# A two-layer attention decode on one core: value products with the probabilities as weights, one-unit loads around the change of batch, and smaller portions of side work

## The chip, the cores and the metric

The kernel runs on one core of a Trainium2 chip. The metric is the time of one execution on that core in microseconds (us). Every comparison below uses fast runs: the granted TensorE clock was 1.00.

## The reference

One new token is decoded for each of eight sequences, through the same attention and feed-forward block twice. Keys and values of 8 sequences x 32 heads x 4096 positions x 128 channels in bf16 are what has to be read: 134 million numbers of each, a second time for the second layer where they are no longer on the chip.

```python
B, Sq, D = 8, 1, 640
Hq, Hkv, Sk, Dh = 32, 32, 4096, 128          # Dff = 1728
...
def reference(A_x, A_k_cache, A_v_cache, A_wq, A_wo, B_x, B_w1, B_w2):
    def _A_ref(x, k_cache, v_cache, wq, wo):
        q = ...                                # x @ wq, one row per head
        scores = jnp.einsum("bhqd,bhkd->bhqk", q, k) * (Dh ** -0.5)
        p = _softmax(scores, axis=-1)
        o = jnp.einsum("bhqk,bhkd->bhqd", p, v)
        return ... @ wo
    def _B_ref(x, w1, w2): ...                 # max(x @ w1, 0) @ w2
    x = A_x
    x = x + _A_ref(_layernorm(x, axis=-1), A_k_cache, A_v_cache, A_wq, A_wo)
    x = x + _B_ref(_layernorm(x, axis=-1), B_w1, B_w2)
    x = x + _A_ref(_layernorm(x, axis=-1), A_k_cache, A_v_cache, A_wq, A_wo)
    x = x + _B_ref(_layernorm(x, axis=-1), B_w1, B_w2)
    return x
```

Both layers read the same cache, and sequences (the text calls each a batch) do not touch each other.

## The kernel before

All weights stay in SBUF. Beside them lies an arena of 22 units of 512 KB, through which the cache streams. The work goes in visits: a visit is one pair of heads of one batch in one layer, with four units of keys and then four of values. A planner in plain Python lays down every load, product and side step in order. Because layer 1 reads what layer 0 has read, the last 16 units of a batch in layer 0 are not freed but used again by layer 1. From then until layer 1 has used them the stream has only 22 - 16 = 6 units to live in. That happens once for each of the eight batches, and the text calls it a dip, after what the transfer rate does there.

The size of a load follows the room that is left:

```python
GPH = 2; UNIT = 2 * GPH; GP = 4; G = 22; SPARE = 6; SMALL = 4; AHEAD = 3   # one line each
...
            keeping = keeps(which, i, g)
            roomy = G - len(kept)
            n = 4 if keeping or roomy >= 16 else 2 if roomy >= SMALL else 1
```

Side work (layer norms, feed-forward, queries of layer 1, output products) waits in chains. Between attention blocks the planner takes one step off every chain, whatever its size:

```python
    def step():
        for c in chains:
            if c:
                ops.append(c.pop(0)[1])
                rest(c)
        ...
        small = G - len(kept) < SMALL
        for g in range(UNIT):
            ops.append(("mm", which, i, g, find(which, i, g)))
            release(which, i, g)
            if g + 1 < UNIT and (g % 2 or small):
                step()
```

One such step may be a whole half of the feed-forward (70 products), or 40 query products. Keys and values both are the stationary operand of TensorE, with one moving column:

```python
        for n in range(GJ):                     # 16 products for each unit
            j = half * GJ + n
            lhsT = arena[:, u * GW + n * P : u * GW + (n + 1) * P]
            if which == "K":
                nc.tensor.matmul(s_tiles[i][:, h, j : j + 1], lhsT=lhsT, rhs=q, start=True, stop=True)
            else:
                nc.tensor.matmul(
                    oy[i][:, h : h + 1], lhsT=lhsT, rhs=P_tiles[i][:, h, j : j + 1],
                    start=(j == 0), stop=(j == NJ - 1),
                )
```

The root of the layer norm is one activation on ScalarE (`func=ACT.Sqrt`), which needs another table than the exponentials (the trace has 49 table loads, 1.28 us each).

## Time and profile before

| | before |
|---|---|
| median of 4 runs | 2524.14 us |
| span of the profiled run | 2523.4 us |
| moved | 1027.07 MB, mean 407 GB/s |
| granted clock | 1.00 |

First, from the page, the busy time of each engine with its share and its number of instructions, and the queue that carries the instructions themselves (packets, MB, share of the 16 transfer engines).

```profile
PE 1385.3 (55%) x40134; PEld 1300.3 (52%) x40134; DVE 320.3 (13%) x1707; ACT 287.9 (11%) x1422; POOL 0.7 (0%) x6
...
q8 instruction: 313, 5.13, 0.8%
```

TensorE has 40,134 products and as many weight loads.

Then the timeline of TensorE in the dip of which the prediction shows the feed-forward part, a little later (start, duration, engine, line, operation, output and inputs, number merged; in brackets the idle time before it and what ended it).

```profile
535.79 1.23 PE L385 MATMUL q_ps<-xq,wq_sb 128*128 128x1 bf16 x40
538.13 0.99 PE L411 MATMUL s_ps<-q,arena 128*128 128x1 bf16 x32 [1.12 <-ACT q L396]
...
542.01 0.37 PE L385 MATMUL q_ps<-xq,wq_sb 128*128 128x1 bf16 x8 [1.61 <-issue]
```

Forty query products stand in one block, the keys wait 1.12 us for the copy behind them, and in the middle of a later block of forty TensorE stands still for 1.61 us with nothing that it is seen to wait for.

### The profile page before, as it was taken

What the parts mean: (1) busy time and instruction counts of PE and PEld (TensorE: products, weight loads), DVE (VectorE), ACT (ScalarE), POOL (GpSimd) and SP (SyncE); (2) the same over time, 40 slices, a digit from 0 to 9 for tenths busy, and PEclk for the clock granted to TensorE, in tenths of its full rate; (3) what the DMA queues carried; (4) which work ended last, traced back from release to release, by engine and by line L of the source; (5) the groups of instructions that cost most, each with busy time, mean ns of one, the idle gap of its engine ahead of it and who ended that gap; (6) DMA issues with size and microseconds to landing.
All of it is one profiled execution on the core that took longest, in us unless ns stands there. A gap on an engine that the chain in (4) does not pass through costs nothing.

```text
span 2523.4 us, 84569 instructions
## 1 busy us (share of the span) xinstructions
PE 1385.3 (55%) x40134; PEld 1300.3 (52%) x40134; DVE 320.3 (13%) x1707; ACT 287.9 (11%) x1422; POOL 0.7 (0%) x6
## 2 busy tenths in 40 slices
PE   3447545475454755557455564555645466445745
PEld 3336545464454744547454564545645455444744
DVE  0001111111111111111111111111111111111111
ACT  1001101010010101101010110101101011000200
POOL 0000000000000000000000000000000000000000
DMA  9999999999999999999999999999999999999897
GB/s 408 425 426 377 414 425 426 424 353 426 426 425 419 362 425 425 425 408 380 426 425 426 395 366 426 425 426 389 402 425 425 425 377 405 426 425 409 325 425 307
DMA packets 82525, 1027.07 MB, mean 407 GB/s; under 512 B 9220, under 2 KB 9220, under 8 KB 9220
## 3 DMA queue, kind: packets, MB, share of 16 engines
q1 hardware_dynamic: 82180, 1021.68, 97.3%
q8 instruction: 313, 5.13, 0.8%
q14 instruction: 32, 0.26, 0.0%
HBM read 1021.63 MB, written 0.01 MB: 405 GB/s over the span
## 4 chain that ended last, share of the span: by engine, by line
DMA 76%; PE 19%; issue 4%; ACT 1%; SPq 0%; DVE 0%; ACTq 0%
DMA arena<-in_A_k_cache_dram 38%; DMA arena<-in_A_v_cache_dram 38%; PE s_ps L411 6%; PE oy_ps L413 6%; PE blk_ps L448 1%; PE q_ps L385 1%; DMA wq_sb<-in_A_wq_dram 1%; PE oy_ps L463 1%; PE ch_ps L334 1%; PE ch_ps L351 1%; PE blk_ps L424 1%; ACT L442 0%; PE blk_ps L433 0%; PE ch_ps L312 0%; ACT P_sb L442 0%
## 5 line engine op out<-in xcount | busy, mean ns | idle before, releaser
L411 PE MATMUL s_ps<-q,arena 128*128 128x1 bf16 x16384 | 518.0, 165 | 586.3 <-DMA arena<-in_A_k_cache_dram 530.4
L413 PE MATMUL oy_ps<-P_sb,arena 128*128 128x1 bf16 x16384 | 520.0, 166 | 509.8 <-DMA arena<-in_A_v_cache_dram 482.8
L411 PEld LDWEIGHTS <-arena 128*128 128x128 bf16 x16384 | 479.7, 104 | 607.6 <-DMA arena<-in_A_k_cache_dram 547.9
L413 PEld LDWEIGHTS <-arena 128*128 128x128 bf16 x16384 | 481.8, 105 | 555.5 <-DMA arena<-in_A_v_cache_dram 500.6
L437 ACT ACTIVATE nmax<-blk_ps 128x2 f32<-128x2 f32 x256 | 44.0, 172 | 1985.0 <-PE blk_ps L433 1985.0
L452 DVE RECIPROCAL invL<-blk_ps 128x2 f32<-128x2 f32 x256 | 43.7, 171 | 966.0 <-PE blk_ps L448 966.0
L428 DVE TENSOR_REDUCE hmx<-blk_ps 2x1 f32<-2x128 f32 x256 | 71.4, 279 | 732.3 <-PE blk_ps L424 732.3
L448 PE MATMUL blk_ps<-lrow,ones_c 128*128 128x2 f32 x512 | 145.3, 353 | 2.5 <-issue 2.5
L442 ACT ACTIVATE P_sb<-s_ps,nmax 128x32 bf16<-128x32 f32 x512 | 142.2, 283 | 7.8
L463 PEld LDWEIGHTS <-wo_sb 128*128 128x128 bf16 x2560 | 131.7, 121 | 7.4 <-issue 7.2
L448 PEld LDWEIGHTS blk_ps<-lrow,ones_c 128*128 128x128 f32 x512 | 128.7, 311 | 4.2 <-issue 2.6
L463 PE MATMUL oy_ps<-oT,wo_sb 128*128 128x1 bf16 x2560 | 104.9, 165 | 6.6 <-issue 5.4
L442 ACT ACTIVATION_READ_ACCUMULATOR P_sb<-s_ps,nmax 128x1 f32 x512 | 100.5, 196 | 0.0
L420 DVE TENSOR_REDUCE mrow<-s_ps 128x2 bf16<-128x64 f32 x256 | 57.6, 225 | 214.3 <-PE s_ps L411 214.3
L424 PE MATMUL blk_ps<-ident,mrow 128*2 128x128 bf16 x256 | 68.4, 267 | 1.5 <-issue 1.3
L456 DVE TENSOR_TENSOR oT<-oy_ps,invL 128x2 bf16<-128x2 f32 x256 | 40.8, 159 | 159.5 <-PE oy_ps L413 159.5
L385 PEld LDWEIGHTS <-wq_sb 128*128 128x128 bf16 x1440 | 43.2, 105 | 14.1 <-issue 10.8
L351 PEld LDWEIGHTS <-w_sb 128*128 128x128 bf16 x1120 | 45.3, 107 | 8.7 <-issue 6.6
L351 PE MATMUL ch_ps<-hT,w_sb 128*128 128x1 bf16 x1120 | 45.9, 168 | 6.1 <-issue 5.7
L470 DVE TENSOR_TENSOR xT<-xT,oy_ps 128x5 f32<-128x5 f32 x256 | 41.0, 160 | 46.8 <-PE oy_ps L463 25.4
L433 PE MATMUL blk_ps<-diag,onesb_c 2*128 2x2 bf16 x256 | 46.8, 183 | 0.0
L385 PE MATMUL q_ps<-xq,wq_sb 128*128 128x1 bf16 x1280 | 40.0, 165 | 10.3 <-issue 10.3
(42 smaller groups left out, 324.7 us busy)
## 6 DMA issues: line engine op xcount, KB each, us to landing
arena<-in_A_v_cache_dram SPq DMA_DIRECT2D x208, 2048.0 KB, 21.9
arena<-in_A_k_cache_dram SPq DMA_DIRECT2D x192, 2048.0 KB, 22.5
arena<-in_A_k_cache_dram SPq DMA_DIRECT2D x96, 1024.0 KB, 8.5
arena<-in_A_v_cache_dram SPq DMA_DIRECT2D x64, 1024.0 KB, 7.1
wq_sb<-in_A_wq_dram SPq DMA_DIRECT2D x4, 1280.0 KB, 25.0
wo_sb<-in_A_wo_dram SPq DMA_DIRECT2D x4, 1280.0 KB, 34.3
w_sb<-in_B_w_dram SPq DMA_DIRECT2D x1, 2240.0 KB, 36.6
w_sb<-in_B_w_dram SPq DMA_DIRECT2D x1, 2160.0 KB
```

What stands on the lines that cost most here:

```text
L351: nc.tensor.matmul(y_ps[:, c : c + 1], lhsT=w2_sb[:fs, f, c * P : (c + 1) * P], rhs=st[key, "hT"][:fs, f : f + 1], start=(f == 0), stop=(f ...
L385: nc.tensor.matmul(q_ps[:, h, :], lhsT=wq_sb[:, g, c, h * Dh : (h + 1) * Dh], rhs=xl[:, c : c + 1] if layer else xl[:, :, c], start=(c == ...
L411: nc.tensor.matmul(s_tiles[i][:, h, j : j + 1], lhsT=lhsT, rhs=q, start=True, stop=True)
L413: nc.tensor.matmul(oy[i][:, h : h + 1], lhsT=lhsT, rhs=P_tiles[i][:, h, j : j + 1], start=(j == 0), stop=(j == NJ - 1),)
L420: nc.vector.tensor_reduce(out=m_tiles[i], in_=s_tiles[i], axis=AX.X, op=ALU.max)
L424: nc.tensor.matmul(blk[i][:2, :P], lhsT=m_tiles.pop(i), rhs=ident, start=True, stop=True)
L428: nc.vector.tensor_reduce(out=hmx, in_=blk[i][:2, :P], axis=AX.X, op=ALU.max)
L433: nc.tensor.matmul(blk[i][:, P : P + 2], lhsT=ones_b, rhs=nmax.pop(i), start=True, stop=True)
L437: nc.scalar.activation(out=nm, in_=blk[i][:, P : P + 2], func=ACT.Copy, scale=-inv_sqrt_dh)
L442: nc.scalar.activation(out=P_tiles[i][:, h, :], in_=S[:, h, :], func=ACT.Exp, bias=nm[:, h : h + 1], scale=inv_sqrt_dh, accum_out=l_tiles[ ...
L448: nc.tensor.matmul(blk[i][:, P + 2 : P + 4], lhsT=ones_f, rhs=l_tiles.pop(i), start=True, stop=True)
L463: nc.tensor.matmul(oy[i][:, 2 + c : 3 + c], lhsT=wo_sb[:, 2 * hp + h, c * P : (c + 1) * P], rhs=o[:, h : h + 1], start=(h == 0), stop=(h = ...
```

## The change

The intent is to get the dips out of the transfer rate. The change has these parts, cut to their core here:

```diff
-SMALL = 4
-AHEAD = 3
+SMALL = 8
+AHEAD = 4
+CAP = 20
...
-            n = 4 if keeping or roomy >= 16 else 2 if roomy >= SMALL else 1
+            n = 4 if roomy >= 16 else 2 if roomy >= SMALL else 1
+            if i == NV - 1 and which == "V":
+                n = 1
...
     def step():
-        for c in chains:
-            if c:
-                ops.append(c.pop(0)[1])
-                rest(c)
+        n = 0
+        for c in sorted(chains, key=lambda c: c[0][0]):
+            if not n or n + c[0][0] <= CAP:
+                n += c[0][0]
+                take(c)
...
-            if g + 1 < UNIT and (g % 2 or small):
+            if g + 1 < UNIT:
                 step()
...
+        if which == "V":
+            for c in range(4):
+                h, j = c // 2, g * VJ + c % 2 * CJ
+                nc.tensor.matmul(
+                    o_ps[32 * c : 32 * c + CJ, :], lhsT=P_tiles[i][:, h, j : j + CJ],
+                    rhs=arena[:, at + c * CJ * Dh : at + (c + 1) * CJ * Dh],
+                    start=(g == 0), stop=(g == UNIT - 1), tile_position=(0, 32 * c),
+                )
+            return
...
+            if nb == 1:
+                inverse_root(rstd, st[key, "var"])     # about 12 small DVE operations
+            else:
+                ... ACT.Sqrt, reciprocal
...
+    up_parts = [range(f, min(f + 3, FC)) for f in range(0, FC, 3)]
...
+        b0, nb = (b, 1) if layer == 0 else (0, B)      # layer 1: one finish for all batches
```

In words: loads of one unit where six are free; at most 20 side products between two units, with the feed-forward cut into portions of 14 or 15 and queries into portions of 10; the first visits of the next batch that come between a batch's two layers are four instead of three; the value product uses four columns of the probabilities as weights in each of four column strips and streams the values, followed by a copy of 100x512 to SBUF and four small gathering products; the root moves from ScalarE to VectorE; the softmax sum becomes a product with ones; layer 1's output products and feed-forward are done once, for all eight batches, at the end. The array of values is laid out on the host to suit (not timed, as before).

## The prediction

> **What bounds the kernel now.** I began with the page's row of slices. It asks one question: is any engine, or the transfer system, full?
>
> ```profile
> PE   3447545475454755557455564555645466445745
> DMA  9999999999999999999999999999999999999897
> GB/s 408 425 426 377 414 425 426 424 353 426 426 425 419 362 425 425 425 408 380 426 425 426 395 366 426 425 426 389 402 425 425 425 377 405 426 425 409 325 425 307
> DMA packets 82525, 1027.07 MB, mean 407 GB/s; under 512 B 9220, under 2 KB 9220, under 8 KB 9220
> ```
>
> TensorE is half idle; the transfers are busy nine tenths of nearly every slice, and most slices stand at 425 or 426 GB/s, the plateau. 1027.07 MB at 426 GB/s are 2411.0 us, so of the span of 2523.4 us 112.4 us are transfer time lost, and no change that keeps the bytes can win more. The losses are eight dips, one in about every five slices, and the end. Next I cut the span into stretches of 40 us and looked around one dip (columns: stretch, its length, busy time of PE, PEld, DVE, ACT, POOL with instructions, granted clock, DMA share, GB/s).
>
> ```profile
> 440.00:480.00 40.00, 19.24 (x568) 18.09 (x568) 4.34 (x23) 3.27 (x20) 0.00 (x0) 1.00 1.01 425
> 480.00:520.00 40.00, 20.15 (x574) 18.66 (x570) 5.45 (x29) 4.56 (x21) 0.00 (x0) 1.00 0.95 391
> 520.00:560.00 40.00, 31.18 (x901) 29.58 (x901) 6.04 (x33) 8.43 (x31) 0.00 (x0) 1.00 0.96 356
> 560.00:600.00 40.00, 23.60 (x690) 22.02 (x686) 5.71 (x30) 4.09 (x25) 0.00 (x0) 1.00 1.00 413
> ```
>
> Where GB/s falls, PE rises to 31 of 40 us. With (426 - GB/s) / 426 x 40 us for each stretch, the eight dips cost 8.9, 11.1, 10.4, 9.3, 13.5, 8.9, 10.1 and 17.4 us: 89.6 in all. The first stretch costs 2.8, the end (2480 on) 17.6; 2.4 are spread thinly. This is the budget.
>
> Why the dips? The plan keeps 16 of the 22 arena units (512 KB each) for the second layer, so around each change of batch the stream lives in 6 units. There the kernel loads 2 units at a time, so three slots. In the same stretch TensorE must do the batch's finish (feed-forward) and the second layer's queries. The timeline of one dip:
>
> ```profile
> 523.93 9.57 SPq L376 DMA_DIRECT2D arena<-in_A_v_cache_dram  x4
> 523.94 2.25 PE L334 MATMUL ch_ps<-xf,w_sb 128*128 128x1 bf16 x70
> 524.24 1.28 ACT L442 ACT_TABLE_LOAD   x1
> 525.53 0.29 ACT L442 ACTIVATE P_sb<-s_ps,nmax 128x32 bf16<-128x32 f32 x1
> ...
> 527.43 1.38 PE L351 MATMUL ch_ps<-hT,w_sb 128*128 128x1 bf16 x33
> 529.05 1.60 PE L351 MATMUL ch_ps<-hT,w_sb 128*128 128x1 bf16 x37 [0.24 <-issue]
> ```
>
> All 70 products of one feed-forward half go out in one block, 2.25 us, then 70 more in about 3.2 us. A 2-unit attention block takes only 1.0 us, so during a block no arena unit comes free, and the queue of loads runs dry. The second cause is in the groups' idle column:
>
> ```profile
> L413 PE MATMUL oy_ps<-P_sb,arena 128*128 128x1 bf16 x16384 | 520.0, 166 | 509.8 <-DMA arena<-in_A_v_cache_dram 482.8 <-issue 26.7
> L411 PE MATMUL s_ps<-q,arena 128*128 128x1 bf16 x16384 | 518.0, 165 | 586.3 <-DMA arena<-in_A_k_cache_dram 530.4 <-issue 46.9 <-ACT q L396 8.9
> L385 PE MATMUL q_ps<-xq,wq_sb 128*128 128x1 bf16 x1280 | 40.0, 165 | 10.3 <-issue 10.3
> ```
>
> "issue" is time in which PE waited for nothing the profile shows: 84 us in these rows, in single gaps of 1 to 3 us, nearly all in the dips. My reading, which I mark as inference, is that instructions arrive late: instructions come through the same transfer engines (queue q8, 5.13 MB), and the gaps follow long runs of back-to-back PE instructions.
>
> **What the Trainium skill says.**
> "TensorE: Matmul & The Clock Gate", Part 3, says products in different column strips run at once and gives 2.38x for three strips at N=512; Part 2 gives a lone warm matmul a gap of N/2.4 + 2.5 ns, so 216 ns at N=512. "TensorEngine Tiling (Array Packing)", Performance Considerations, recommends just this swap of stationary and streaming operand when the moving side is thin. The trace before has no such product, so it can't say; its thin pairs run at 1.01 us per 32, 32 ns each.
> "ScalarE: Activation LUTs", What ACT_TABLE_LOAD costs, gives 1283 ns per load; the trace agrees exactly (49 loads, mean 1283 ns).
> "DMA: Bandwidth & Descriptors", SWDGE vs HWDGE vs iDMA, measured 408.7 GB/s for one load stream with 4 KiB rows. This trace's loads have rows of 8 and 16 KB; whole bins of 16 KB rows reach 426, the best of 8 KB rows about 420.
>
> **The change part by part.**
> *Value products turned round.* Per unit, 16 pairs (weights from V, one column) become 4 pairs (weights from P, 4 columns; moving 512 columns of V), each in its own column strip. Before: 0.52 us a unit. After: about 0.3 us if the strips overlap, 4 x 216 = 0.86 us if not (estimates from the skill). Added per visit: a copy of 100x512 by ACT (estimate 0.7 us, extrapolated from the 128x64 copy's 212 ns) and 4 thin gather pairs on PE (0.13 us plus latency). Neither lies on the load path in the steady state, where PE waits 2.3 to 2.7 us for each load.
> *PE instructions.* Listed per engine, 79,352 become 52,866. At 64 B (5.39 MB of instruction traffic over 84,569 instructions) that removes 1.7 MB, 4.0 us of plateau transfer, less a little for added DVE work: 4 us on the path, because the transfers are the path.
> *Softmax sum.* 512 fp32 passes of 353 ns become 256 bf16 products of 64 columns; 512 accumulator reads of 196 ns leave ACT; one more 0.2 us reduction per visit on DVE. All hidden.
> *Layer norm.* Square root moves from ACT to about 12 small DVE operations of about 0.16 us, 2.5 us with gaps; 46 of 49 table loads go. The plan puts an empty step behind it, but a maximum queued behind it on DVE can hold PE for about 1.7 us, twice a dip. Six single units give slack: a freed unit may return late by 5 x 1.23 us less about 1.8 us of transfer latency, about 4.3 us. So covered.
> *Second layer's finish once for all eight batches.* 7 feed-forwards (980 pairs) and 1120 output pairs go. Most lay in plateau stretches (360 to 400 us is at 425 GB/s), so they were free; only the last dip, which holds two finishes, profits.
> *Pacing.* The blocks of 70 become parts of 14 or 15, and queries come 10 at a time; at most 20 products stand between two units. PE time per unit: 0.3 to 0.5 us of attention plus up to 0.66 us, against 1.23 us per unit at 426 GB/s. Over four visits (32 units) the transfer needs 39.4 us. PE needs: K 16 x 0.52 = 8.3, V 16 x 0.3 = 4.8 (13.8 if serial), 140 + 160 pairs x 33 ns = 9.9, norms 4 x 0.57 = 2.3, small work 4. Together 29 (38 if serial). Before, the 31 us of PE in 40 us also fitted on average; it was the lumps and gaps that lost.
> *Smaller loads.* 260 loads of one unit (4 KB rows), nearly all in the dips. From the packets, 8 KB rows take 309 ns and 16 KB 613, so a row costs about 5 ns extra; with the gap per load I estimate 1.3 us per dip.
> *End.* The last values come unit by unit (saves about 1.5 us), the copy and gather cost about 1 us. 17.6 becomes about 17.
>
> Sum: bytes 1025.4 MB / 426 = 2407; start 2.8; spread 2.4; end 17; dips 8 x 2.5 = 20 (1.3 small loads, 1.2 leftover waits). That is 2449 of span; run times lie about 0.7 above. **Predicted 2450 us**, 2.9% less.
>
> **The rivals.**
> (a) *The small loads don't hold the plateau.* For: 4 KB rows at the skill's 408.7 GB/s, one issue of 0.33 us for each, 32 in a dip. Against: 0.33 is far below 1.23 us, and 8 KB rows lose little. It would cost 3 to 5 us per dip: about 2465.
> (b) *The strips don't overlap, or run at a slow array clock.* 38 of 39.4 us leaves no room for waits, so dips stay at 7 to 9 us: 2490 to 2505. Against: the skill's measured overlap, and the granted clock stands at 1.00.
> (c) *The gaps called issue stay.* They took 84 us on PE in all. If they depend on time since the last pause and not on the number of instructions, 5 us a dip remain: about 2470.
> (d) *The new copy becomes a wait.* One o_ps bank: the copy must end before the next values, one key block away, at least 2 us. Unlikely to show.
> (e) *Nothing is lost in the dips:* 2430.
>
> **Range and chances.** Most weight lies on dips of 1 to 6 us: 2435 to 2480. 2% is at about 2474, which means 5.6 us per dip; about four fifths lie below. Faster 0.82, within 2% 0.165, slower 0.015 (only if the serial strips also hurt the steady state). Range 2432 to 2482.
>
> **What would show it.** Slices at the dips should read 405 to 420 GB/s instead of 353 to 395. The idle column of the key and value products should show issue of 40 us or less in place of 74. A value unit should take 0.3 us, its four products starting nearly together; 0.8 us would prove rival (b). One-unit loads landing at clearly over 1.23 us apart with units free would prove (a). Issue gaps of the old size inside the dips would prove (c). A plateau other than 425 would overturn the whole sum.

## The result, and the profile after

| | before | after | predicted |
|---|---|---|---|
| median | 2524.65 us (13 runs, with those of later rounds) | 2467.20 us (8 runs, 2466.06 to 2468.24) | 2450 |
| ratio | | 0.9775 (0.9765 to 0.9785) | 0.971 |
| span | 2523.4 | 2464.8 | 2449 |

A ratio is the mean time of one kernel's fast runs over the mean of the other's fast runs of the same rounds, so it is not quite the ratio of the two medians. The change is faster by 2.25%, outside the 2% band, inside the predicted range (2432 to 2482), and 17 us slower than the predicted time. Of an expected gain of 74 us, 57 came. The record lists a ninth run of the kernel after, 2468.76 us, that its median leaves out.

The page after, its busy times, the rate in 40 slices, the bytes and the instruction queue:

```profile
PE 1282.4 (52%) x26486; PEld 794.4 (32%) x26486; DVE 381.5 (15%) x1984; ACT 337.3 (14%) x1179; POOL 0.7 (0%) x6
...
GB/s 406 425 426 405 420 427 425 424 397 425 426 426 423 392 426 426 426 421 397 426 427 425 413 410 427 426 426 404 411 426 426 426 405 418 426 426 412 410 425 305
DMA packets 105896, 1025.38 MB, mean 416 GB/s; under 512 B 11829, under 2 KB 11829, under 8 KB 45109
...
q8 instruction: 207, 3.39, 0.6%
```

The plateau of 425 to 427 GB/s has not moved. The eight low places are still there and read 392 to 413 where they read 325 to 395. TensorE has a third fewer products, and instructions take 1.74 MB less.

The stretches around the dip that the prediction shows (columns as there):

```profile
480.00:520.00 40.00, 23.45 (x491) 15.58 (x492) 8.54 (x47) 4.88 (x16) 0.00 (x0) 1.00 0.99 396
520.00:560.00 40.00, 34.67 (x763) 24.17 (x760) 9.57 (x52) 8.48 (x38) 0.00 (x0) 1.00 1.02 410
```

391 and 356 GB/s have become 396 and 410, though TensorE is busier there than before (34.67 of 40 us against 31.18): a fuller engine, and a better fed stream. What counts in the dip is not how much work there is but how long one piece of it can hold up the next free unit.

The budget, made as in the prediction from stretches of 40 us:

| us | before | predicted | after |
|---|---|---|---|
| bytes at 426 GB/s | 2411.0 | 2407 | 2407.0 |
| eight dips | 89.6 | 20 | 33.5 |
| start | 2.8 | 2.8 | 2.8 |
| end | 17.6 | 17 | 17.5 |
| thinly spread | 2.4 | 2.4 | 4.0 |
| span | 2523.4 | 2449 | 2464.8 |

So 13.5 of the 16 us that the span is above its prediction lie in the dips, 4.2 us for each instead of 2.5.

The value, key and query groups after (columns: busy time and mean ns, then idle time before them with its causes):

```profile
L460 PE MATMUL o_ps<-arena,P_sb 128*4 128x512 bf16 x4096 | 557.4, 606 | 579.1 <-DMA arena<-in_A_v_cache_dram 573.6
L472 PE MATMUL s_ps<-q,arena 128*128 128x1 bf16 x16384 | 536.4, 165 | 544.2 <-DMA arena<-in_A_k_cache_dram 534.0
...
L444 PE MATMUL q_ps<-xq,wq_sb 128*128 128x1 bf16 x1280 | 53.8, 166 | 3.6 <-issue 2.9
```

Next to nothing but transfers is left in the idle column. "Issue" is 2.9 us here in the queries; the list of waits adds 7.6 for the keys and 3.5 for the values (sum, number, longest):

```profile
PE s_ps L472 <- issue: 7.6, 11, 1.6
PE o_ps L460 <- issue: 3.5, 3, 2.0
```

Those 14 us stand against 84 before in the same three groups. But look at the busy time of the values: 557.4 us for 1024 units are 0.54 us a unit, no less than the 520.0 us of before.

The timeline of the dip shows both how the portions lie between units and what still holds a unit up:

```profile
514.80 0.16 PE L491 MATMUL blk_ps<-diag,onesb_c 2*128 2x2 bf16 x1 [0.95 <-DVE diag L488]
514.89 0.56 PE L376 MATMUL ch_ps<-xf,w_sb 128*128 128x1 bf16 x15
515.38 0.60 PE L460 MATMUL o_ps<-arena,P_sb 128*4 128x512 bf16 x4
515.91 0.56 PE L376 MATMUL ch_ps<-xf,w_sb 128*128 128x1 bf16 x15
516.40 0.60 PE L460 MATMUL o_ps<-arena,P_sb 128*4 128x512 bf16 x4
...
2426.68 1.02 PE L460 MATMUL o_ps<-arena,P_sb 128*4 128x512 bf16 x8
```

Fifteen feed-forward products, a unit of values, fifteen, a unit: one unit comes free about every microsecond. In front of it TensorE has waited 0.95 us for a small product on VectorE, which was queued behind the new root. The last line is from the steady state: two units of values back to back take 1.02 us, 0.51 each.

The loads after (number, KB each, median us from issue to landing):

```profile
arena<-in_A_v_cache_dram SPq DMA_DIRECT2D x132, 512.0 KB, 7.1
arena<-in_A_k_cache_dram SPq DMA_DIRECT2D x128, 512.0 KB, 7.5
```

These are the 260 one-unit loads. From the completion records in the trace I took, for each load, the time at which the last of the 16 transfer engines reported, and the distance from one load to the next where loads follow without a pause. One unit of 512 KB then takes 1.276 us in one-unit loads (rows of 4 KB), 1.2465 in two-unit loads (8 KB) and 1.226 in four-unit loads (16 KB). That sizes the tax of small loads in a dip: 32 units x 0.05 us and 24 more in pairs x 0.02 are 2.1 us. The rest of the 4.2, again 2.1 us, is what the small loads do not explain. I count it as waits here; what stays open, further down, says how much of it may be none. The prediction had 1.3 and 1.2.

### The profile page after: what moved, and what is told of

Read it like the earlier page. It is cut to its first block, busy times and chain, and to the rows that moved or that the text cites. A ratio compares the mean times of both kernels' runs of the same rounds, so it can differ in the third digit from the quotient of the medians.

```text
span 2464.8 us, 57629 instructions
## 1 busy us (share of the span) xinstructions
PE 1282.4 (52%) x26486; PEld 794.4 (32%) x26486; DVE 381.5 (15%) x1984; ACT 337.3 (14%) x1179; POOL 0.7 (0%) x6
## 2 busy tenths in 40 slices
DMA packets 105896, 1025.38 MB, mean 416 GB/s; under 512 B 11829, under 2 KB 11829, under 8 KB 45109
## 4 chain that ended last, share of the span: by engine, by line
DMA 83%; PE 13%; DVE 2%; issue 1%; ACT 0%; SPq 0%; ACTq 0%
DMA arena<-in_A_k_cache_dram 43%; DMA arena<-in_A_v_cache_dram 41%; PE s_ps L472 5%; PE o_ps L460 5%; PE q_ps L444 1%; DVE hmx L486 1%; ACT o_sb L518 0%; PE oy_ps L523 0%; PE oy_ps L540 0%; DVE diag L488 0%; PE blk_ps L491 0%; PE blk_ps L482 0%; PE blk_ps L504 0%; PE ch_ps L393 0%; PE ch_ps L376 0%
## 5 line engine op out<-in xcount | busy, mean ns | idle before, releaser
L460 PE MATMUL o_ps<-arena,P_sb 128*4 128x512 bf16 x4096 | 557.4, 606 | 579.1 <-DMA arena<-in_A_v_cache_dram 573.6
L472 PEld LDWEIGHTS <-arena 128*128 128x128 bf16 x16384 | 493.0, 104 | 578.2 <-DMA arena<-in_A_k_cache_dram 568.9
L460 PEld LDWEIGHTS <-P_sb 128*4 128x4 bf16 x4096 | 109.8, 83 | 684.6 <-issue 678.3
L518 ACT CAST o_sb<-o_ps 100x512 bf16<-100x512 f32 x256 | 149.8, 585 | 124.3 <-PE o_ps L460 124.3
L510 DVE TENSOR_REDUCE lsum<-blk_ps 128x2 f32<-128x64 f32 x256 | 57.5, 225 | 422.1 <-PE blk_ps L504 422.1
L504 PEld LDWEIGHTS <-onesb_c 128*128 128x128 bf16 x256 | 26.5, 103 | 203.7 <-issue 203.7
L523 PE MATMUL oy_ps<-gsel,o_sb 100*128 100x2 bf16 x1024 | 63.5, 166 | 3.5 <-ACT o_sb L518 0.7
L504 PE MATMUL blk_ps<-P_sb,onesb_c 128*128 128x64 bf16 x256 | 59.9, 234 | 1.1 <-ACT P_sb L499 1.1
L540 PE MATMUL oy_ps<-oT,wo_sb 128*128 128x1 bf16 x1280 | 51.8, 165 | 0.0
L540 PEld LDWEIGHTS <-wo_sb 128*128 128x128 bf16 x1440 | 50.9, 105 | 0.8 <-issue 0.8
```

Of the source, the lines that this page charges most:

```text
L460: nc.tensor.matmul(o_ps[32 * c : 32 * c + CJ, :], lhsT=P_tiles[i][:, h, j : j + CJ], rhs=arena[:, at + c * CJ * Dh : at + (c + 1) * CJ * D ...
L472: nc.tensor.matmul(s_tiles[i][:, j : j + 1], lhsT=arena[:, at + n * P : at + (n + 1) * P], rhs=q, start=True, stop=True)
L504: nc.tensor.matmul(blk[i][:, P + 2 :], lhsT=ones_p, rhs=P_tiles[i].rearrange("p h j -> p (h j)"), start=True, stop=True)
L518: nc.scalar.copy(out=o_tiles[i][:OR], in_=o_ps[:OR, :].rearrange("p (j d) -> p j d", j=CJ))
L523: nc.tensor.matmul(oy[i][:, :2], lhsT=o_tiles[i][:OR, j, :], rhs=gsel[:OR, j, :], start=(j == 0), stop=(j == CJ - 1))
L540: nc.tensor.matmul(oy[i][:, 2 + c * nb : 2 + (c + 1) * nb], lhsT=wo_sb[:, 2 * hp + h, c * P : (c + 1) * P], rhs=o1[:, 2 * hp + h, :] if la ...
```

## The experiments

Each was compared with the kernel before in the same rounds; the distance to the kernel after is between medians (2467.2). In these rounds the kernel before had medians of 2524.35 to 2525.70 us, so such a distance is good to 1 or 2 us. All results were correct. There are two questions: which part of the change earns the time, and what holds the rest of the dips.

### Single loads undone

```diff
-SMALL = 8
+SMALL = 4
```

> The changed kernel, but with two-unit loads (1 MB) in place of one-unit loads (512 KB) where the arena is short. Theory load tax: the trace after shows a unit landing every 1.276 us with one-unit loads, 1.247 with two-unit and 1.226 with four-unit loads, so 32 units a dip x 0.03 x 8 dips = 8 us are won and the time falls to about 2459 us. Theory slack: what made the dips short is that one-unit loads leave the tensor engine more slack before the queue runs dry; then the dips grow from 4.2 us to 6 to 8 us each and the time rises to 2480 to 2497 us.

Measured: 2494.69 us, ratio 0.9881 (0.9862 to 0.99): 27 us more than after. In the same dip, on TensorE:

```profile
525.42 0.62 PE L376 MATMUL ch_ps<-xf,w_sb 128*128 128x1 bf16 x10
527.72 0.60 PE L460 MATMUL o_ps<-arena,P_sb 128*4 128x512 bf16 x4 [1.67 <-DMA arena<-in_A_v_cache_dram]
```

The values now come 1.67 us late, and the stretch 520 to 560 carries 371 GB/s instead of 410. Six units in pairs are three slots, and a slot is asked for again only when both units are read. Small loads cost transfer time, and earn more than they cost.

### Single loads alone, in the kernel before

```diff
-SMALL = 4
+SMALL = 8
```

> The kernel before with one constant changed (one-unit loads, and a chain step after each unit, where under 8 units are free); all the rest as before. Theory slack: most of the gain is finer loads, so the dips fall from 11.2 to about 6 us and the time to about 2480 us. Theory lumps and gaps: the blocks of 70 products and the issue gaps remain, so the dips stay at 9 to 11 us and the time at 2505 to 2525 us.

Measured: 2549.79 us, ratio 1.0095 (1.0079 to 1.0111): 25 us slower than before, which neither theory had. In the kernel before the same constant also decides that side steps come after each unit instead of each pair, and a wait that was not there appears in the list of waits (sum, number, longest):

```profile
PE s_ps L411 <- issue: 48.8, 33, 2.5
PE blk_ps L448 <- ACT P_sb L442: 30.4, 32, 1.7
```

The softmax sum is asked for too early behind the exponentials, 32 times. The issue gaps stay, and so do the blocks of 70. So this run has two edits in one and does not price single loads cleanly. What it does show is that the constant whose undoing costs 27 us in the new kernel brings no gain in the old one, with the steps that come along with it.

### Blocks of 70 again

The cap is lifted and each half of the feed-forward is one step; queries stay in portions of 10, but nothing limits what is put together.

```diff
-CAP = 20
+CAP = 1000
...
-    up_parts = [range(f, min(f + 3, FC)) for f in range(0, FC, 3)]
-    visits, ops = plan(B, NP, len(up_parts), DC)
+    up_parts = [range(FC)]
+    visits, ops = plan(B, NP, len(up_parts), 1)      # "down" loops over c inside
```

> The changed kernel with the feed-forward in two blocks of 70 products again and no cap on the products per step. Theory pacing: the lumps made the dips; they grow from 4.2 to 7 or 8 us and the time rises to 2490 to 2500 us. Theory slack: six single units tolerate about 4 us, a block takes 2.3 to 3 us, so each block costs under 1 us: 2470 to 2480 us.

Measured: 2509.61 us, ratio 0.9937 (0.9919 to 0.9954): 42 us more than after, more than the pacing theory gave. One stretch and three lines of the timeline:

```profile
520.00:560.00 40.00, 31.69 (x720) 22.79 (x720) 8.66 (x48) 8.49 (x38) 0.00 (x0) 1.00 0.93 343
```

```profile
520.10 2.25 PE L376 MATMUL ch_ps<-xf,w_sb 128*128 128x1 bf16 x70
522.28 0.60 PE L461 MATMUL o_ps<-arena,P_sb 128*4 128x512 bf16 x4
522.81 2.83 PE L394 MATMUL ch_ps<-hT,w_sb 128*128 128x1 bf16 x70
```

TensorE does about as many products in the stretch as after (720 against 763), but only one unit comes free between 520.1 and 525.6 us, while the stream can fill four in that time (5.5 / 1.276); the rate falls to 343 GB/s. The issue gaps of TensorE came to 0.6 us in this whole run. So lumps do the harm without any help from the issue gaps. Part of the 42 us may be a further wait that this plan makes: output products up to 2.2 us behind their input, 15.5 us in seven waits.

### Values as weights again

The value product, its layout and two output buffers as before; no copy, no gather. All the rest of the change stays. The diff is shortened.

```diff
-            for c in range(4):
-                ... lhsT=P_tiles[i][:, h, j : j + CJ], rhs=arena[...512 columns...], tile_position=(0, 32 * c)
+            for n in range(GJ):
+                nc.tensor.matmul(oy[i][:, h : h + 1], lhsT=arena[:, at + n * P : at + (n + 1) * P],
+                                 rhs=P_tiles[i][:, h, j : j + 1], ...)
```

> The changed kernel with the value products as before (weights from V, one column each), layout of V as before, no copy and no gather. 24 thousand more tensor engine instructions: 1.6 MB more instruction traffic, 3.7 us of plateau, in any case. Theory issue gaps: idle put down to issue on the key and value products returns from 11 us to over 50, dips grow to 7 us, time 2490 to 2500 us. Theory that pacing alone did it: dips stay at 4 to 5 us and the time at 2470 to 2475 us.

Measured: 2508.72 us, ratio 0.9931 (0.9916 to 0.9946): 41 us more than after, above the 2490 to 2500 of the issue theory. From its list of waits, and its instruction queue:

```profile
PE s_ps L471 <- issue: 37.4, 22, 2.9
PE oy_ps L460 <- issue: 26.1, 13, 2.4
```

```profile
q8 instruction: 295, 4.83, 0.8%
```

The issue gaps are back: 63.5 us in keys and values (73.6 before) and 74 in all lines of the list (103 before), though pacing, loads and the finish are those of the new kernel. They reach the transfers: in the dip shown above, gaps of 2.65, 2.09 and 2.13 us end at 551, 558 and 569 us, and the stretch 565 to 570 carries 256 GB/s with the transfer engines busy for 0.63 of it (426 and 1.01 after). So it is the value product with its many instructions, and not the blocks of 70, that brings them back. The number is not all: with the same number of instructions they came to 14 us in the kernel after and to 0.6 in the run with blocks of 70, so how the work is spaced counts as well. The instruction traffic itself (1.44 MB more, 3.4 us at 426 GB/s) is a small part of the 41 us.

What the gaps are can be taken one step further. The packets of the instruction queue are 16,384 B, which are 256 instructions of 64 B. 313 packets x 256 are 80,128 in the kernel before, where TensorE has 80,268 instructions with its weight loads; 207 x 256 are 52,992 after, for 52,972. So this queue feeds TensorE. Of the gaps of over 1 us that are put down to issue, 64 on the weight loads before and 31 in this run, the end came a median 1.38 us after the end of one of those transfers, with the middle half before within 1.30 to 1.45 us; points picked at random lie 0.3 to 9 us behind one, median about 4. As I read it, TensorE is waiting for its next instructions there. That is an inference from timing, a strong one; no run slows the fetch alone.

### The root on ScalarE again

```diff
-            if nb == 1:
+            if False:
                 inverse_root(rstd, st[key, "var"])
```

> The changed kernel with the square root of the single-batch norms on ACT again (two table loads of 1.28 us each around it). Theory that the move was covered and idle: in the trace after PE waits 7 us in all for the maximum queued behind the root on DVE; that goes, and the table loads lie beside other work, so the time stays within 4 us of 2467. Theory that the table loads fed the dips: the exponentials come 2.6 us later twice a dip, the dips grow by 2 us or more each, and the time is above 2483 us.

Measured: 2470.12 us, ratio 0.9782 (0.9768 to 0.9797); after is 0.9775 (0.9765 to 0.9785). The intervals overlap. The moved root, with 32 table loads saved (35 in this run, 3 after) and its 0.95 us waits for VectorE gained, does next to nothing. What it gains and what it costs were not taken apart.

### One-unit loads everywhere

```diff
-            n = 4 if roomy >= 16 else 2 if roomy >= SMALL else 1
+            n = 1
```

> The changed kernel with one-unit loads everywhere, also where the arena is roomy and nothing waits. Theory load tax: a unit lands every 1.276 us instead of 1.226, so 1468 units now loaded by fours cost 0.05 us each and 192 now loaded by twos 0.03 us: 79 us more, about 2546 us, and the plateau falls to 409 GB/s. Theory that 1.276 is only the short queue of the dips: the plateau stays at 426 and the time at 2460 to 2475 us.

Measured: 2551.95 us, ratio 1.0107 (1.0092 to 1.0122), as the tax of 0.05 us a unit has it (2546). A stretch of the steady state:

```profile
640.00:680.00 40.00, 20.43 (x343) 11.55 (x340) 4.45 (x22) 4.33 (x16) 0.00 (x0) 1.00 1.03 409
```

Rows of 4 KB hold 408 to 409 GB/s here, far from any dip. This run also separates the two halves of a dip. As all its loads are of one unit, a dip cannot be lower than its surroundings by load size. Against a plateau of 408.5 its eight dips still lose 1.5 to 2.7 us, 16.8 in all, 2.1 each. That is the leftover found above by subtraction.

### More kept, less room

```diff
-SPARE = 6
+SPARE = 5      # 17 units kept; and in a second run 4, 18 kept
```

> The changed kernel with 17 units kept and 5 left for the stream. Saves 8 loads of 0.52 MB, 9.8 us of plateau. By the slack sum (5 units: 4 x 1.23 less 1.8 = 3.1 us in place of 4.3) the waits of PE in the dips, the longest about 2 us, still fit: about 2457 us. If the slack is already used up, each dip grows by 1.5 us or more and the time is 2468 us or above.

> 18 units kept, 4 left for the stream. Saves 19.7 us of plateau; the slack falls to 1.9 us, under the longest wait. If the dips grow by less than 2.4 us each, this beats the changed kernel (down to 2448 us); by the slack sum they grow by 3 us or more: 2472 us and above.

Measured: 2490.1 us, ratio 0.986 (0.9845 to 0.9875), and 2528.3 us, ratio 1.0022 (1.0005 to 1.0038). One more kept unit saves 8 x 0.524 MB, which are 9.8 us at 426 GB/s. So waits grew by 33 us with five units, and by 81 with four. The room was not generous at six.

The slack can be worked out now. Across all traces but that of the last run below (3.99 us) the shortest time from issue to the landing of a one-unit load was 4.03 us, seen in the run with blocks of 70; the earliest that the first of the 16 engines was done with a load was 2.65 us. Less its own 1.28 us of transfer, that is a latency of 2.75 us. A unit may then come free late by 5 x 1.276 - 2.75 = 3.6 us with six units, 2.35 with five and 1.08 with four (estimates from these numbers). With pairs in three slots it is about 2 x 2.49 - 2.75 = 2.2 us, which fits that the first experiment and the run with five units look alike (27 and 33 us).

### Layer 1 finished for each batch

The output products, norm and feed-forward of layer 1 are done batch by batch, as before, with the new pacing.

```diff
-            if layer == 0 or b == B - 1:
+            if True:
                 chains[-1] += [(10, ("W", i)), (0, ("Y", i))]
...
-        b0, nb = (b, 1) if layer == 0 else (0, B)
+        b0, nb = b, 1
```

> The changed kernel with the second layer's output products, norm and feed-forward done for each batch as it ends, as before, instead of once for all eight. Theory of the prediction: most of it lies in plateau stretches and is free; 4,200 more tensor engine instructions are 0.27 MB, 0.6 us, and the last dip, where two finishes meet, may grow by up to 7 us: 2468 to 2475 us. Rival: the seven finishes cost 2 us or more each where they lie: above 2481 us.

Measured: 2478.47 us, ratio 0.9819 (0.9805 to 0.9832): 11 us more than after, 3 above the range. Seven feed-forwards and 1120 output products came back. Between 2240 and 2360 us, the last dip, this run loses 11.3 us against 4.4 after; the rest is 1 us or less here and there and 1.5 at the end. Work in the plateau is nearly free; work in a dip is not.

### Fewer kept, more room

```diff
-SPARE = 6
+SPARE = 7      # 15 units kept; and in a second run 8, 14 kept, where loads go in pairs by the rule
```

> The changed kernel with 15 units kept and 7 left for the stream. Eight more loads cost 9.8 us of plateau for certain. Going from 6 spare units to 5 and 4 cost 33 and 81 us beyond the bytes; if what is left in the dips (4.2 us each, 2.1 of it load tax) is still such waits, a seventh unit wins back up to 16 us: 2461 to 2470 us. If the waits left at 6 units are of another kind, nothing comes back: 2475 to 2479 us.

> 14 units kept, 8 left; by the kernel's own rule the loads in the dips are then pairs. 19.7 us more bytes; load tax falls by 8 us; four pair slots give a slack of 3 x 2.46 less 1.8 = 5.6 us, more than six single units. If all waits vanish, 2463 us; if they stay as they are, 2479 us; if pair loads are harmful in themselves, as with 6 units (27 us), above 2490 us.

Measured: 2479.1 us, ratio 0.9822 (0.9808 to 0.9835), and 2478.8 us, ratio 0.9821 (0.9807 to 0.9834). With seven units the time rises by 11.9 us, and 9.8 of these are the reloaded bytes. None of the waits was won back. The rate in slices with seven units:

```profile
GB/s 407 424 425 405 425 425 425 423 389 426 426 426 422 398 426 426 425 420 399 426 426 426 407 412 426 426 426 402 418 426 426 426 400 413 426 426 412 409 426 297
```

The dips have the same depth as with six (389 to 412). So the leftover of about 2 us a dip is not for want of units. With eight units in pairs, 19.7 us of bytes cost only 11.6: the tax of single loads is won back, 8 us, and pairs do no harm where there are four slots.

### Three visits ahead

```diff
-AHEAD = 4
+AHEAD = 3
```

> The changed kernel with three visits of the next batch ahead of the second layer instead of four, the one constant of the change not yet tried alone. Eight fewer one-unit loads per dip save 0.4 us of load tax each, 3 us in all. Theory that the fourth visit only makes room for the chain: with three, the last down product, the second norm with its root and the first query are forced out in one go before the first second-layer visit, a stop of PE of about 6 us against a slack of about 3.6 us (six slots of 1.276 us less the shortest time from issue to landing seen, 4.03 us), so the dips grow by 2 to 4 us each: 2480 to 2500 us. Rival: in that stretch kept units cover the stop, and the time is 2464 to 2468 us.

Measured: 2504.77 us, ratio 0.9911 (0.9895 to 0.9928): 38 us more than after. A new wait stands in its list:

```profile
PE q_ps L444 <- DVE xq L342: 21.4, 8, 2.7
```

With smaller portions the chain of feed-forward, norm and queries takes longer from end to end, and needs four visits of the next batch to be stretched over. With three, layer 1 asks for its queries before the chain is through, the planner empties the rest of it at once, and TensorE waits up to 2.7 us in each of the eight batches. A stretch of 351 GB/s in place of 410 follows. The one number that looks like tidying in the diff is a part of the pacing.

I also planned an arena of 23 units with 16 kept. It did not fit in SBUF, so it was not run. The new softmax sum and the unit-wise loads of the last values were not undone by themselves. No version that ran is faster than the kernel after.

## Why the prediction was right, and where it was off

What was right, by its own steps:

- **The budget.** The plateau stayed at 425 to 427 GB/s, bytes came out at 1025.38 MB (1025.4 predicted), start and end at 2.8 and 17.5 us (2.8 and 17). Working from the bytes upward made the prediction robust: everything uncertain lay in one term of 20 us.
- **Dips from lumps and from issue gaps.** Each comes back without the other: blocks of 70 bring 42 us back with 0.6 us of issue gaps, the old value product brings 41 us and the gaps back with the new pacing.
- **Issue depends on the number of instructions.** The gaps fell from 84 to 14 us; keys and values kept 11 of 74, where up to 40 was allowed. Rival (c) is out. That the instructions come late stays an inference, and their spacing counts too.
- **Norm and finish.** The moved root is worth nothing measurable, and the finish once for all is worth 11 us, of which about 7 in the last dip, which is where the prediction said.
- **The copy.** Measured at 585 ns against an estimate of 0.7 us. It became a wait twice, for 0.5 and 0.7 us, both at the very end. Rival (d) is out.

What was off:

- **"dips 8 x 2.5 = 20 (1.3 small loads, 1.2 leftover waits)"** measured 33.5, or 4.2 each. The small loads were sized from packet durations with an estimated gap; landings show 2.1 us. By the prediction's 5 ns a row a row of 4 KB would take 157 ns; it took 161. Rival (a) was right in kind (408 to 409 GB/s with 4 KB rows), but its 3 to 5 us a dip were too many. The leftover measured 2.1 us, by subtraction and again in the run with one-unit loads everywhere. So the slices at the dips read 392 to 413 GB/s, below the 405 to 420 that were to show it.
- **"about 4.3 us. So covered."** took a latency of about 1.8 us, for which the prediction gives no source and no trace here shows one; the shortest landings give 2.75, so the slack was 3.6. The runs with five and four units show how near the edge that is: 33 and 81 us of waits.
- **"After: about 0.3 us if the strips overlap"** measured 0.51 (half of the 1.02 us of two units; from the start of one to the start of the next it is 0.38), with little or no gain over before. The four strips of a unit do start together (within 10 ns in three quarters of the units), so rival (b)'s serial 0.86 us is refuted as well; but the next four start only about 380 ns later. The conclusion held for another reason than the one written down: the swap pays by having fewer instructions, not by a faster unit.
- **The parts do not add.** The sum treated pacing, loads and instruction count as separate savings. Undone one at a time, pacing takes back 42 us, the value product 41, the fourth visit ahead 38 and single loads 27: 148 together out of a gain of 57. The reading that fits is that they protect the same slack: when any one of them uses it up, the dips are back. Single loads put alone into the old kernel made it slower by 25 us, if with the side effect told there.
- **"run times lie about 0.7 above"** compared a median with the span of another run. A run's own time lies 1.7 to 1.8 us above its span (2525.13 and 2523.4, 2466.55 and 2464.8), so this step was 1 us short.

What stays open: the cause of the leftover 2.1 us in each dip. It is not the number of units: a seventh did not reduce it. The issue gaps that remain are not cleared: every dip has some, 14 us in all. In the dip shown above they cannot be what lowers the rate, though: they end at 547 and 554 us, and the rate is lowest from 500 to 520 us (385 and 358 GB/s in its two halves). The 0.95 us waits for VectorE, 6.9 us in all, are a candidate; moving the root back to ScalarE did not help, but that run brings table loads back, so it does not clear them.

About half of what looks like loss may be none. When a dip begins, the 16 transfer engines finish one load 5 to 7 us apart (3.5 in the first dip), some 20 us later 2.4 to 3.1 us: the faster ones use up a lead that had been counted as rate before. A load has landed only when its last engine is done. So I counted, on the last engine alone, how far the loads of a dip landed behind the paces of 1.276, 1.2465 and 1.226 us, less what the loads outside the dips lose in the same length of time. That is 0.8 to 1.2 us a dip in the kernel after, depending on where a dip is cut off, against about 7 in the kernel before and 5.7 with blocks of 70. This is read from the completion records, and no run tests it. The thin spread of 4.0 us against 2.4 was not followed up.

## What to carry to other kernels

When a stream runs through few buffers, work out how late a buffer may come free (buffers less one, times the time of one load, less the latency, which is to be read from the shortest issue-to-landing in the trace), and then cut all other work on the engine that frees buffers into pieces well below that; total busy time can rise and the kernel still gain. Try changes that guard the same slack together, since one of them alone may show nothing. And count the instructions of the busiest engine: where it stands still for 1 to 3 us without a visible cause, look whether instruction packets end just before it goes on.

## What the Trainium skill lacked or had wrong

- "TensorE: Matmul & The Clock Gate", Part 3: that products in different column strips run at once agrees (four start within 10 ns in three quarters of the units). The pace of such groups is not lacking there, I read it wrongly: I took Part 2's 216 ns for a lone product of 512 columns, but Part 3 gives a group the whole duration of one product plus about 4 ns for each further tile. The next four started about 380 ns after the first, and two units took 1.02 us.
- "DMA: Bandwidth & Descriptors", SWDGE vs HWDGE vs iDMA: 408.7 GB/s with 4 KiB rows agrees (408 to 409 GB/s with one-unit loads everywhere). A row of figures by row length for such loads is lacking; the runs show 1.276, 1.2465 and 1.226 us for 512 KB with rows of 4, 8 and 16 KB.
- "DMA: Bandwidth & Descriptors", Anatomy of one DMA: its fixed cost of about 2.0 us, given there for the software path, is too little to plan a full queue by. The shortest one-unit load took 4.03 us from issue to landing, 2.75 without its own transfer, and the 16 engines finished a one-unit load 2.2 to 6.7 us apart in the run after, half of the loads 2.8 to 3.9; no page gives that distance.
- "Runtime: NRT & Kernel Launch", Instruction fetch mechanics: blocks of 256 instructions that come over a DMA queue agree (207 packets of 16,384 B for 52,972 instructions). It calls the cost of a block mostly hidden. If the gaps are late instructions, as their timing says, that did not hold here: 84 us of such gaps with 80,268 instructions, 14 us with 52,972.
